# Loading r and k by feature in two transfers of 48 partitions

## The chip, the cores and the metric

The kernel runs on one core of one Trainium2 chip. The metric is device time of the whole kernel in microseconds (us): the median of several executions, and, for the profile, one execution recorded instruction by instruction. PE is TensorE (matrix products), PEld its weight loads, DVE VectorE, ACT ScalarE, POOL GpSimd, SP the engine that issues most of the transfers (DMAs); SPq is SP's queue.

## The reference

Three blocks run one after the other on 3,072 tokens (4 sequences of 768, 8 heads of 48 features, so 384 features per token).

```
# attention, for every sequence and head, t = 0..767, state starts at 0 (48 x 48)
y[t]  = r[t] @ (state + outer(u * k[t], v[t]))
state = w[:, None] * state + outer(k[t], v[t])

# mixture of experts: one of 8 experts per token
e = argmax(x @ w_gate);  p = softmax(x @ w_gate)[e];  g = sigmoid(x @ w_output_gate)[e]
x = p * g * (relu(x @ w1[e]) @ w2[e])          # 384 -> 1024 -> 384

# gated feed-forward
out = (silu(x @ w_gate2) * (x @ w_val)) @ w_out # 384 -> 1536 -> 384
```

## The kernel before

The attention works on 24 tiles of 128 tokens (6 per sequence). Within a tile it uses the form with powers of the decay: r is multiplied by powers of w, k by their inverses, and matrix products give the scores of all pairs of tokens of the tile; a 48 x 48 state per head carries over to the next tile.

For that, each tile needs r and k in two layouts. By token: partition = token, free axis = head and feature (`tok`, 384 KB of r and k per tile, line 342; v is loaded apart, line 346). By feature: partition = feature, free axis = pair of heads and token (`tr`, line 341). Two heads share the 128 partitions: head 0 of a pair has partitions 0 to 47, head 1 partitions 64 to 111. Partitions 48 to 63 and 112 to 127 are rows of zeros, written on the host into `tr`, so that a half always has 64 rows. The products read all 64 rows of a half (lines 496 and 552), so these rows must be zero, not merely unused.

The inputs of a tile land in one of three buffers, `io[i % NIO]` with `NIO = 3`; v has four buffers of its own. `load(i + NIO)` is called in `scaled_r(i)`, as soon as tile i's r and k have been read for the last time.

In this stage the order of every engine's work is the order in which the code is written (`manual_schedule`), SP's too. One round of the loop issues, among others: on POOL `ck` (two products, lines 455 and 456), `kdT` (line 458) and `kdc` (line 460); on DVE `rdT` (line 467), the sums `cb` from `ck` (line 479), the masked copy of the scores (line 500), the state (line 528), and pieces of the routing of the experts (lines 131 to 273); on ACT the diagonal blocks `dsb` (line 483) and copies; on SP the loads of a later tile, the store of the finished rows `x_d` (line 127), and in some rounds weights of the first expert (lines 1050 and 1054), which ACT and DVE split in two parts (lines 1062 and 1065). After the stage come the experts and the feed-forward, ordered by a planner from estimated times.

Of the kernel before, what the change touches and what calls it, by code (L numbers as in the profile page):

```python
# [20 lines left out]
P = 128  # L21
# [17 lines left out]
def moe_kernel(ctx, tc, cst, small, tok, tr, u, w1, w2, m_gate, m_val, m_out, out):  # L39
    nc = tc.nc  # L40
    NT, DM = out.shape
    H, D = u.shape
# [35 lines left out]
    rows = const.tile([P, E * NJ], I32, name="rows")  # L78
# [227 lines left out]
    with ExitStack() as actx:  # L306
# [26 lines left out]
        RK, V, T = 2 * H * D, H * 64, NP * P  # L333
        NIO, NV = 3, 4
# [3 lines left out]
        def load(i):  # L338
            if i < NTILE:
                t = io[i % NIO]  # L340
                nc.sync.dma_start(out=t[:, RK:], in_=tr[i])
                nc.sync.dma_start(out=t[:, 0:RK], in_=tok[i, :, 0:RK])

        def load_v(i):
# [8 lines left out]

        u_tok = carve(H * D).rearrange("p (h d) -> p h d", d=D)
        load(0)
        nc.sync.dma_start(out=u_tok, in_=u.rearrange("(o h) d -> o h d", o=1).to_broadcast([P, H, D]))
        nc.sync.dma_start(out=cs, in_=cst)
        for i in range(1, NIO):
            load(i)
            load_v(i - 1)  # L360
# [101 lines left out]
        def scaled_r(i):  # L462
            if i >= NTILE:
                return
            r_t, k_t, rT, kT, rdT, kdT, ck, kdc = S[i]
            if i:
                nc.vector.tensor_tensor(out=rdT, in0=rT, in1=wr_ps, op=ALU.mult)
            if i == 1:
                load_v(3)
            load(i + NIO)  # L470
            if i == 0:
                load_v(2)
# [1065 lines left out]
```

## Time and profile before

| | us |
|---|---|
| median of 3 runs | 815.05 |
| lowest and highest of them | 812.76, 816.62 |
| the profiled execution, device time | 815.9 |
| its span, first to last instruction | 814.1 |
| TensorE busy in the span | 780.3 |
| VectorE busy | 509.8 |
| GpSimd busy | 206.9 |

The profiled execution is one of its own, so sums over its rows are compared with its 815.9 us. Busy shares are means over stages that differ: the attention fills about the first 126 us, the experts follow to some 360 us, then the feed-forward. A DMA share is the mean busy share of the core's 16 DMA engines; it can come out slightly above 1.

### The profile page before, as it was taken

What the parts mean: (1) busy time and instruction counts of PE and PEld (TensorE: products, weight loads), DVE (VectorE), ACT (ScalarE), POOL (GpSimd) and SP (SyncE); (2) the same over time, 40 slices, a digit from 0 to 9 for tenths busy, and PEclk for the clock granted to TensorE, in tenths of its full rate; (3) what the DMA queues carried; (4) which work ended last, traced back from release to release, by engine and by line L of the source; (5) the groups of instructions that cost most, each with busy time, mean ns of one, the idle gap of its engine ahead of it and who ended that gap; (6) DMA issues with size and microseconds to landing.
All of it is one profiled execution on the core that took longest, in us unless ns stands there. A gap on an engine that the chain in (4) does not pass through costs nothing.

```text
span 814.1 us, 15597 instructions
## 1 busy us (share of the span) xinstructions
PE 780.3 (96%) x5982; PEld 716.5 (88%) x5983; DVE 509.8 (63%) x1091; ACT 347.9 (43%) x791; POOL 206.9 (25%) x203
## 2 busy tenths in 40 slices
PE   6999879699999999999999999999999999999997
PEld 3888778599999999998888888888888888899997
DVE  7799997288999899879564335333533533344443
ACT  5878763275665666565432112222221221222321
POOL 6999951345323422221002000200010020001000
PEclk9999999799999999999999999999999999999999
DMA  8899933665778777454311000000000010001000
GB/s 319 311 355 349 333 129 115 218 211 160 235 261 258 239 240 231 129 179 155 109 38 43 10 1 14 39 1 0 14 40 1 5 42 1 1 8 40 1 20 24
DMA packets 61859, 99.27 MB, mean 122 GB/s; under 512 B 5461, under 2 KB 48105, under 8 KB 61776
## 3 DMA queue, kind: packets, MB, share of 16 engines
q1 hardware_dynamic: 58320, 88.34, 32.9%
q0 software_dynamic: 3456, 9.85, 3.6%
q8 instruction: 49, 0.80, 0.4%
q14 instruction: 34, 0.28, 0.1%
HBM read 81.64 MB, written 16.53 MB: 121 GB/s over the span
## 4 chain that ended last, share of the span: by engine, by line
issue 52%; PE 23%; POOL 3%; DVE 2%; DMA 1%; another core or an unknown queue 1%; ACT 1%; POOLq 0%; SPq 0%; ACTq 0%; DVEq 0%
PE ph L1190 9%; PE py L1190 9%; POOL out_dram L1362 2%; PE pt L1156 1%; DMA rw<-m 1%; PE pha L1190 1%; PE ph L1186 1%; PE pya L1190 1%; POOL x L1033 1%; PE py L1186 1%; DMA m<-x 0%; POOLq L1379 0%; PE ph L1187 0%; DVE wl L968 0%
## 5 line engine op out<-in xcount | busy, mean ns | idle before, releaser
L1386 PE MATMUL pg<-x,wh 128*128 128x512 f32 (+1 forms) x504 | 146.5, 358 | 0.0
L1391 DVE TENSOR_TENSOR hv<-pg,hv 128x512 f32<-128x512 f32 (+1 forms) x84 | 51.6, 614 | 143.2 <-ACT hv L1390 143.0
L1386 PE MATMUL pv<-x,wh 128*128 128x512 f32 (+1 forms) x504 | 137.7, 358 | 0.0
L1362 POOL DMA_INDIRECT out_dram<-ot,tokd x24 | 24.9, 1037 | 407.3 <-DVE ot L1361 402.9
L1390 ACT ACTIVATE hv<-pg 128x512 f32<-128x512 f32 (+1 forms) x84 | 45.0, 536 | 160.1 <-PE pg L1386 159.7
L967 ACT CAST hh<-hv 128x512 fp32r<-128x512 f32 (+1 forms) x84 | 47.0, 560 | 136.0 <-DVE hv L1392 136.0
L1386 PEld LDWEIGHTS pv<-x,wh 128*128 128x128 f32 x504 | 89.9, 188 | 13.9
L1386 PEld LDWEIGHTS pg<-x,wh 128*128 128x128 f32 x504 | 90.2, 188 | 11.3
L1353 PE MATMUL po<-wh,hl 128*128 128x384 f32 x288 | 97.1, 338 | 0.0
L1353 PE MATMUL po<-wl,hh 128*128 128x384 f32 x288 | 96.8, 336 | 0.0
L1353 PE MATMUL po<-wh,hh 128*128 128x384 f32 x288 | 96.8, 336 | 0.0
L1386 PE MATMUL pg<-x,wl 128*128 128x512 f32 (+1 forms) x252 | 90.3, 358 | 0.0
L1386 PE MATMUL pv<-x,wl 128*128 128x512 f32 (+1 forms) x252 | 90.3, 358 | 0.0
L1190 PE MATMUL ph<-x,w1h 128*128 128x416 f32 (+6 forms) x336 | 87.4, 340 | 0.0
L1190 PE MATMUL py<-h,w2h 128*128 128x416 f32 (+6 forms) x336 | 83.0, 341 | 0.0
L968 DVE TENSOR_TENSOR hl<-hv,hh 128x512 fp32r<-128x512 f32 (+1 forms) x84 | 51.7, 615 | 43.9 <-ACT hh L967 43.6
L1392 DVE TENSOR_TENSOR hv<-pv,hv 128x512 f32<-128x512 f32 (+1 forms) x84 | 51.7, 615 | 39.0 <-PE pv L1386 38.6
L483 ACT ACTIVATE dsb<-cs,cb 128x128 f32<-128x128 f32 x192 | 58.8, 389 | 21.0 <-DVE cb L479 21.0
L1190 PEld LDWEIGHTS ph<-x,w1h 128*128 128x128 f32 x336 | 61.4, 188 | 0.1
L1190 PEld LDWEIGHTS py<-h,w2h 128*128 128x128 f32 x336 | 60.7, 188 | 0.5 <-DVE h L1210 0.3
L1190 PE MATMUL ph<-x,w1l 128*128 128x416 f32 (+6 forms) x168 | 58.3, 347 | 0.4 <-DVE h L1210 0.4
L1033 POOL TENSOR_TENSOR low<-low,exw 128x384 f32<-128x384 f32 x30 | 33.5, 1118 | 96.1 <-DVE exw L1029 78.7
(248 smaller groups left out, 1511.2 us busy)
## 6 DMA issues: line engine op xcount, KB each, us to landing
r<-in_w_dram SPq DMA_DIRECT2D x64, 384.0 KB
yd_all<-in_tr_dram SPq DMA_DIRECT2D x24, 512.0 KB
yd_all<-in_tok_dram SPq DMA_DIRECT2D x24, 384.0 KB
rw<-m SPq DMA_DIRECT2D x36, 192.0 KB
yd_all<-in_tok_dram SPq DMA_DIRECT2D x24, 256.0 KB
m<-ab SPq DMA_DIRECT2D x30, 192.0 KB
x_d<-xt SPq DMA_DIRECT2D x24, 192.0 KB
cva<-in_w_gate_dram SPq DMA_DIRECT2D x10, 384.0 KB
```

The source lines that it names most:

```text
L483: nc.scalar.mul(dsb[:, h, :], ident, cb[:, h : h + 1])
L967: first = nc.scalar.copy(hi, src)
L968: second = nc.vector.tensor_tensor(out=lo, in0=src, in1=hi.bitcast(F32), op=ALU.subtract)
L1033: nc.gpsimd.tensor_tensor(out=low, in0=low, in1=ex.bitcast(F32), op=ALU.mult)
L1186: nc.tensor.matmul(dst[:, 0 : 2 * n], lhsT=hi, rhs=x, start=start, stop=False, skip_group_check=True)
L1190: nc.tensor.matmul(dst[:, 0:n], lhsT=a, rhs=b, start=start and t == 0, stop=stop and t == 2)
L1353: mm = nc.tensor.matmul(po[t], lhsT=a[:, t * P : (t + 1) * P], rhs=bb, start=(f == 0 and j == 0), stop=(f == KF2 - 1 and j == 2))
L1362: st = nc.gpsimd.indirect_dma_start(out=out[:, :], out_offset=bass.IndirectOffsetOnAxis(ap=tokd[:, i : i + 1].bitcast(U32), axis=0), in_=o ...
L1386: nc.tensor.matmul(dst, lhsT=a[:, fs], rhs=bb[:, q, :], start=(q == 0 and j == 0), stop=(q == KD - 1 and j == 2))
L1390: nc.scalar.activation(hv, pg, AF.Sigmoid)
L1391: nc.vector.tensor_tensor(out=hv, in0=pg, in1=hv, op=ALU.mult)
L1392: nc.vector.tensor_tensor(out=hv, in0=pv, in1=hv, op=ALU.mult)
```

## The change

The loads of r and k by feature of the first three tiles, which are the first to fill each of the three buffers, stay as they were and bring the zero rows. From the fourth tile on, the load is issued as two: partitions 0 to 47 and partitions 64 to 111. The rows of zeros are then not loaded again; they stay in the buffers. Nothing else in the program is edited.

```
         def load(i):
             if i < NTILE:
                 t = io[i % NIO]
-                nc.sync.dma_start(out=t[:, RK:], in_=tr[i])
+                rows = [slice(0, P)] if i < NIO else [slice(0, D), slice(P // 2, P // 2 + D)]
+                for pr in rows:
+                    nc.sync.dma_start(out=t[pr, RK:], in_=tr[i, pr])
                 nc.sync.dma_start(out=t[:, 0:RK], in_=tok[i, :, 0:RK])
```

Here P is 128 and D is 48.

## Rows read from the trace of the kernel before

**Rows 1.** The page, the span in 40 slices of 20.4 us, busy tenths.

```profile
DVE  7799997288999899879564335333533533344443
DMA  8899933665778777454311000000000010001000
```

**Rows 2.** Busy time by stretch; last three columns granted clock, DMA share, GB/s.

```profile
10.00:40.00 30.00, 24.31 (x483) 21.78 (x482) 24.07 (x59) 23.43 (x74) 28.66 (x31) 0.94 0.94 341
40.00:90.00 50.00, 45.17 (x1030) 40.24 (x1028) 47.24 (x139) 40.28 (x124) 46.69 (x45) 1.00 1.00 359
90.00:110.00 20.00, 16.82 (x354) 14.45 (x351) 19.24 (x58) 15.53 (x48) 18.03 (x16) 1.00 0.80 270
110.00:126.00 16.00, 13.07 (x299) 11.71 (x293) 14.34 (x53) 9.07 (x29) 4.02 (x4) 1.00 0.22 68
148.00:157.00 9.00, 1.09 (x8) 0.89 (x7) 0.00 (x0) 1.02 (x3) 5.25 (x7) 0.74 1.04 374
...
55.00:60.00 5.00, 4.11 (x92) 3.67 (x92) 4.90 (x18) 3.59 (x11) 4.28 (x5) 1.00 1.05 413
```

**Rows 3.** Waits of POOL from 55 to 126 us: total, times, longest.

```profile
POOL ck L455 <- DMA yd_all<-in_tok_dram: 3.7, 5, 1.3
```

**Rows 4.** Waits of DVE, first 40 to 55 us, then 55 to 126 us.

```profile
DVE cb L479 <- POOL ck L456: 1.2, 3, 0.5
...
DVE bank L241 <- ACT eo L237: 1.2, 3, 0.4
DVE x L968 <- ACT x L967: 0.9, 1, 0.9
DVE cb L479 <- POOL ck L456: 0.5, 1, 0.5
```

**Rows 5.** Timeline of POOL: start, duration, instruction (tiles 12, 17, 18, 23).

```profile
56.35 1.00 POOL L455 TENSOR_TENSOR ck<-yd_all 128x384 f32<-128x384 f32 x1 [0.64 <-DMA yd_all<-in_tok_dram]
57.43 1.00 POOL L456 TENSOR_TENSOR ck<-ck,yd_all 128x384 f32<-128x384 f32 x1
...
80.08 1.01 POOL L456 TENSOR_TENSOR ck<-ck,yd_all 128x384 f32<-128x384 f32 x1
...
83.58 1.00 POOL L455 TENSOR_TENSOR ck<-yd_all 128x384 f32<-128x384 f32 x1 [1.26 <-DMA yd_all<-in_tok_dram]
84.66 1.00 POOL L456 TENSOR_TENSOR ck<-ck,yd_all 128x384 f32<-128x384 f32 x1
...
108.56 1.00 POOL L455 TENSOR_TENSOR ck<-yd_all 128x384 f32<-128x384 f32 x1 [1.00 <-DMA yd_all<-in_tok_dram]
109.63 1.01 POOL L456 TENSOR_TENSOR ck<-ck,yd_all 128x384 f32<-128x384 f32 x1
```

**Rows 6.** Timeline of DVE: "cb" of tiles 11, 12, 17, 18, 23.

```profile
54.51 0.55 DVE L479 TENSOR_REDUCE cb<-ck 128x8 f32<-128x384 f32 x1 [0.50 <-POOL ck L456]
...
60.41 0.55 DVE L479 TENSOR_REDUCE cb<-ck 128x8 f32<-128x384 f32 x1
...
83.78 0.54 DVE L479 TENSOR_REDUCE cb<-ck 128x8 f32<-128x384 f32 x1
...
91.22 0.54 DVE L479 TENSOR_REDUCE cb<-ck 128x8 f32<-128x384 f32 x1
...
115.94 0.55 DVE L479 TENSOR_REDUCE cb<-ck 128x8 f32<-128x384 f32 x1
```

**Rows 7.** First piece of the chain of waits that ended last.

```profile
128.29 0.85 issue
```

**Rows 8.** DMA issues of r and k by feature, with size.

```profile
yd_all<-in_tr_dram SPq DMA_DIRECT2D x24, 512.0 KB
```

**Rows 9.** Timeline of SP's queue: two issues of a load by feature.

```profile
70.57 0.33 SPq L341 DMA_DIRECT2D yd_all<-in_tr_dram  x1
...
75.92 1.82 SPq L341 DMA_DIRECT2D yd_all<-in_tr_dram  x1
```

**Rows 10.** Longest wait of SP's queue up to 130 us.

```profile
SPq L127 <- ACT lh L129: 49.9, 22, 6.1
```

## Prediction

> **What bounds the kernel now.** I read the page's slices first, then busy time by stretch, then who waited for whom, then single instructions. The edit touches only the loads of the attention stage, so the reader is to see there which engine sets the pace and whether a late load reaches it.
>
> The slices [rows 1] show DMA at 8 or 9 tenths in the first five slices (to about 102 us), and little of it in the last half. In finer stretches [rows 2] the 16 DMA engines are busy 0.94 of 10 to 40 us, 1.00 of 40 to 90 us, and 0.80 of 90 to 110 us. At first sight the stage is short of DMA, and taking bytes away should help.
>
> But full DMA engines need not be what the end waits for. GpSimd (POOL) is the first reader of a tile's loads. From 55 to 126 us it waited for a load 5 times, 3.7 us in all [rows 3]. VectorE (DVE) stands behind POOL: its row sum "cb" (L479) reads the "ck" that POOL made. DVE is busy 47.24 of the 50 us from 40 to 90, 19.24 of the next 20 and 14.34 of the next 16 [rows 2]. Its own waits in 55 to 126 us are 0.5 us for POOL, 1.2 and 0.9 us for ScalarE (ACT), and none for a load [rows 4]. The one wait for POOL ended at 54.51 [rows 6], before the first late load (tile 12, whose POOL work began at 56.35 after 0.64 us of waiting [rows 5]).
>
> So from about 55 us to the end of the stage DVE runs its list without a stop, and POOL is ahead of it. How far ahead is read from one tile in both lists [rows 5, 6]. Counting L456 and L479 along the tiles:
> - tile 12: POOL ends at 57.43 + 1.00 = 58.43, DVE takes it up at 60.41: 1.98 us spare, after a load that came 0.64 late.
> - tile 17: 80.08 + 1.01 = 81.09 against 83.78: 2.69 spare, its load not late.
> - tile 18: 84.66 + 1.00 = 85.66 against 91.22: 5.56 spare, after the latest load of all (1.26).
> - tile 23: 109.63 + 1.01 = 110.64 against 115.94: 5.30 spare, after 1.00.
>
> Every late load of the kernel before dies in this spare time. The chain of waits itself begins only at 128.29 [rows 7], after the stage, and doesn't reach back; the argument therefore rests on DVE's list.
>
> **The change, part by part.**
>
> *Bytes.* One load of r and k by feature is 512 KB [rows 8], 128 rows of 4 KB. Two of 48 rows carry 384 KB: 128 KB (131,072 bytes) less in each of the 21 tiles from the fourth on, 2.75 MB in all. At 413 GB/s, the rate of 55 to 60 us at full DMA [rows 2], 512 KB take 1.27 us and 128 KB 0.32 us. If time went by bytes, the stage would need 21 x 0.32 = 6.7 us less of DMA time. What it is worth to the end: POOL would lose some or all of its 3.7 us of waiting, and DVE, which waits for none of it, would gain 0. Earlier than 55 us POOL never waits for one of the changed loads, so there is nothing to gain either. The term is 0.
>
> *One more transfer per tile.* SP issues 21 instructions more. An issue takes 0.33 us when SP is free, at worst 1.82 [rows 9]. Queued behind it on SP are the tile's token load (r and k by token), the v load and the store of x. The token load is what POOL asks for first, so it starts 0.33 us later, at worst 1.82. SP has the time: it stood 49.9 us before the store of x (L127) waiting for ACT [rows 10]. A token load that is so much later is a fixed delay, not one that adds up, and the smallest spare above is 1.98 us. The cost is 0; without that cover it would be 0.33 us once (at worst 1.82), as DVE would run that much later throughout. The two halves also write the same buffer that the one load wrote, so they wait for the same readers, and the readers now wait for two arrivals in place of one. The rows that aren't loaded keep the zeros that the first three tiles brought.
>
> *How fast a transfer to 48 partitions runs.* Every load of this stage that the trace shows fills 128 partitions; none shows 48. I bound it. Let x be what a tile's two halves together take of DMA time beyond the 1.27 us of the whole one. Lower end: by bytes, x = -0.32. Upper end: each half, although it carries 3/8 of the bytes, holds the engines as long as the whole load did, x = +1.27. The nearest row is the whole load itself: same 4 KB rows, same source and queue, only fewer of them; by it a transfer goes by its rows, and I take a value in the lower part of the range, between -0.32 and the middle (+0.48).
>
> [...]
>
> *What x costs.* From tile 3 to tile n the DMA engines owe (n - 2) times x more. Idle DMA time pays back: 0.06 x 30 = 1.8 us in 10 to 40 us, 0 in 40 to 90, 0.20 x 20 = 4.0 us in 90 to 110 [rows 2]. What is left goes first into DVE's spare time. So DVE is late by
> - tile 12: 10x - 1.8 - 1.98 = 10x - 3.8;
> - tile 17: 15x - 1.8 - 2.69 = 15x - 4.5;
> - tile 23: 21x - 5.8 - 5.30 = 21x - 11.1.
> (The spares above were measured after the late loads, so those are in them.) DVE has no idle time to make good what it loses, so the largest of these counts. At x = -0.32 all are below 0, cost 0. At the middle, 0.48: 1.0, 2.7 and below 0. At 1.27: 8.9, 14.6 and 15.6 us. To come to 4.1 us (0.5% of 815, about what a measurement of this kernel can tell from no change), x must be (4.1 + 4.5)/15 = 0.57.
>
> **Sum.** Bytes 0, issue 0, x in the lower part of its range 0. The profiled execution took 815.9 us for a span of 814.1, with 1.8 us around it; so 815.9 - 0 on its own scale. It stands 0.85 us above the median of the runs, 815.05, so I forecast 815.0.
>
> **The rivals.**
>
> *Slower: the halves are slow.* Place: the DMA engines between 40 and 90 us, share 1.00, no idle time there. Mechanism: a half writes fewer partitions, so if what limits a load is the side that takes the data, 16 engines push into half of it. For it: engines that are equally full move different amounts (359 GB/s at share 1.00 in 40 to 90 us, 413 at 1.05 in 55 to 60 us [rows 2]), so bytes alone don't set a transfer's time. Against it: nothing in the trace has such a shape. It decides from x = 0.57 on. In the middle of 0.57 and 1.27, at 0.92, tile 17 gives 15 x 0.92 - 4.5 = 9.3 us: 824.4 us; at its worst 815.05 + 15.6 = 830.7. [...]
>
> *Faster: POOL sets the pace after all.* DVE's few waits for POOL between 40 and 55 us sum to 1.2 us [rows 4]; if loads were behind these too, and all 3.7 us of POOL's waiting for loads came through to the end, the gain would be 4.9 us: 810.2 us. Against it: those three waits come before any late load, and from 55 us on DVE has work in hand. This is the largest gain I can find.
>
> *The change does nothing that can be seen, although it does what it says.* This is my forecast, not a rival; DMA share falls and DVE's list ends when it did. Within it, a gain of up to 1.2 us or a loss at x up to 0.57 is possible: 811 to 819 us.
>
> *The work after the stage moves.* [...] The edit moves no load of that stretch, so I give it no chance of its own, only part of the ends.
>
> **How the numbers follow.** My forecast 0.57 (811 to 819 us). Halves slow enough to decide 0.34 (819 to 831): no row supports it, but no row excludes it, and the threshold lies at 0.57 in a range up to 1.27. Faster by over 4.1 us 0.09. For 8 in 10 I leave out 0.07 below and 0.13 above: 812 to 826 us; the upper end is x of about 1.0 (15 x 1.0 - 4.5 = 10.5). Faster 0.09, within 0.5% 0.57, slower 0.34.
>
> **What would show it.** Right: POOL's waits for loads below 3.7 us, DMA share of 40 to 90 us below 1.00, about 0.92 by bytes (11 tiles x 0.32 = 3.5 us of 50), bytes moved down by 2.75 MB; DVE's idle time in 55 to 126 us as before, and its last "cb" at about 115.9 us. Wrong through slow halves: DMA share still 1.00 while GB/s fall below 359, POOL's waits for loads of 10 us and more, DVE waiting for POOL in tiles 12 to 17, last "cb" later than 119 us. Wrong through a gain: last "cb" before 112 us. If the last "cb" stays and the time moves, it is the stretch after the stage.

## Result and the profile after

The changed kernel is slower: 818.96 us (median of 10 runs, 816.51 to 822.01) against 813.23 us (10 runs, 810.90 to 816.62) on the same chip. The ratio is 1.0068, 95% interval 1.0051 to 1.0084, so some 5.5 us (4 to 7). I had forecast 815.0, with a chance of 0.57 on no change. The time lies inside the range (812 to 826), but on the rival's side of the 0.5%: "the halves are slow".

The profiled execution took 819.2 us for a span of 817.4. Its line numbers are two higher from the edit on (L455 is now L457, L479 is L481). First the page: the DMA slices of 20.4 us, the packets of the whole execution, and the queue that SP's loads use.

```profile
DMA  8999953665687778365311000000000010001000
GB/s 280 283 299 305 294 176 117 229 196 171 213 281 228 248 230 260 110 190 155 99 57 43 10 1 14 39 1 0 14 39 1 3 43 1 1 8 40 1 20 24
DMA packets 61523, 96.52 MB, mean 118 GB/s; under 512 B 5797, under 2 KB 48441, under 8 KB 61440
...
q1 hardware_dynamic: 57984, 85.59, 34.2%
```

The kernel before had:

```profile
DMA packets 61859, 99.27 MB, mean 122 GB/s; under 512 B 5461, under 2 KB 48105, under 8 KB 61776
...
q1 hardware_dynamic: 58320, 88.34, 32.9%
```

The 2.75 MB are gone as worked out, yet the engines are no less busy: in the sixth slice (102 to 123 us), which holds the end of the loads, DMA now shows 5 tenths against 3 [rows 1]. The busy time by stretch says it plainly (columns as in [rows 2]):

```profile
10.00:40.00 30.00, 25.63 (x520) 23.01 (x524) 23.80 (x60) 23.02 (x75) 28.02 (x30) 0.94 1.04 296
40.00:90.00 50.00, 45.55 (x971) 40.23 (x963) 43.79 (x131) 39.82 (x122) 41.91 (x40) 0.97 1.05 300
90.00:110.00 20.00, 17.09 (x343) 14.92 (x342) 19.42 (x50) 13.94 (x44) 19.04 (x17) 0.91 1.06 297
110.00:126.00 16.00, 11.94 (x257) 10.72 (x259) 15.05 (x60) 9.40 (x32) 9.28 (x9) 1.00 0.35 110
```

From 40 to 90 us the engines are full (1.05, before 1.00) and carry 300 GB/s in place of 359. The idle DMA time that was to pay back, 0.06 of 10 to 40 us and 0.20 of 90 to 110 us [rows 2], is gone. DVE is busy 43.79 of the 50 us, before 47.24.

Who waited for whom, POOL and then DVE, from 55 to 126 us (total, times, longest):

```profile
POOL ck L457 <- DVE bank L210: 2.9, 1, 2.9
POOL ck L457 <- DVE lg L131: 2.7, 1, 2.7
POOL ck L457 <- DMA yd_all<-in_tok_dram: 1.8, 2, 1.1
...
DVE cb L481 <- POOL ck L458: 2.4, 4, 1.4
```

DVE waits 2.4 us for POOL, before 0.5 [rows 4]. By the names in this list POOL's waits for loads went down, 3.7 us [rows 3] to 1.8, and POOL now waits for DVE. The names mislead here. Two waits of POOL, in tiles 12 and 18:

```profile
58.98 0.99 POOL L457 TENSOR_TENSOR ck<-yd_all 128x384 f32<-128x384 f32 x1 [2.66 <-DVE lg L131]
...
89.98 0.99 POOL L457 TENSOR_TENSOR ck<-yd_all 128x384 f32<-128x384 f32 x1 [2.87 <-DVE bank L210]
```

The rows name DVE, which signals after nearly every instruction (1,038 signals, 1,091 instructions in this execution) and did so at 58.91 and 89.95 us, just ahead of the two starts. But all that "ck" needs from DVE is the buffer of the "ck" two tiles earlier, and DVE had read that by 51.60 and 81.62 us. The token loads of the two tiles landed at 58.85 and 89.85 us (times of their signals in the trace), and POOL began 0.13 us behind each. It began 0.13 us behind the landing in tiles 15 and 21 too, whose waits are named for the load. So all of these were waits for loads, and so was one of 0.65 us in tile 16. Counted by landings, POOL waited 8.0 us for loads from 55 to 126 us, before 4.0.

DVE's "cb" of tiles 11, 12, 15, 16, 17, 18 and 23:

```profile
55.13 0.56 DVE L481 TENSOR_REDUCE cb<-ck 128x8 f32<-128x384 f32 x1 [0.46 <-POOL ck L458]
61.09 0.55 DVE L481 TENSOR_REDUCE cb<-ck 128x8 f32<-128x384 f32 x1
...
76.14 0.55 DVE L481 TENSOR_REDUCE cb<-ck 128x8 f32<-128x384 f32 x1 [1.38 <-POOL ck L458]
81.07 0.55 DVE L481 TENSOR_REDUCE cb<-ck 128x8 f32<-128x384 f32 x1 [0.42 <-POOL ck L458]
85.91 0.55 DVE L481 TENSOR_REDUCE cb<-ck 128x8 f32<-128x384 f32 x1 [0.18 <-POOL ck L458]
93.38 0.54 DVE L481 TENSOR_REDUCE cb<-ck 128x8 f32<-128x384 f32 x1
...
119.12 0.55 DVE L481 TENSOR_REDUCE cb<-ck 128x8 f32<-128x384 f32 x1
```

The last one starts at 119.12, before 115.94 [rows 6]: 3.18 us late. The span is 3.3 us longer, so in this pair of executions the stage accounts for all of it, and nothing is added behind the stage. (The pair shows less than the medians: the kernel before's execution, 815.9 us, was 2.7 us above its later median of 813.23.)

The durations of the packets on queue q1 in the first 126 us, read from the trace by size, show where the engines' time went. In this stretch the 4 KB packets are the loads by feature, 3 KB the token loads and 2 KB the loads of v; the edit touches only the first. The sum of the durations is divided by the 16 engines:

```
packet bytes   before: mean ns, sum us    after: mean ns, sum us
4096           184, 35.2                  221, 33.2
3072           134, 25.6                  182, 34.9
2048            88, 16.9                  113, 21.7
```

The loads by feature themselves took 2.0 us less in all, with the halves, than before. The 9.3 and 4.8 us more fell on the token loads and the loads of v, which run beside them.

### The profile page after: what moved, and what is told of

Its sections match the earlier page's. It is cut to its first block, busy times and chain, and to the rows that moved or that the text cites. A ratio compares the mean times of both kernels' runs of the same rounds, so it can differ in the third digit from the quotient of the medians.

```text
span 817.4 us, 15634 instructions
## 1 busy us (share of the span) xinstructions
PE 784.2 (96%) x5982; PEld 719.3 (88%) x5983; DVE 510.2 (62%) x1091; ACT 348.2 (43%) x791; POOL 208.4 (25%) x203
## 3 DMA queue, kind: packets, MB, share of 16 engines
q1 hardware_dynamic: 57984, 85.59, 34.2%
## 4 chain that ended last, share of the span: by engine, by line
issue 53%; PE 14%; DVE 6%; POOL 4%; DMA 3%; ACT 2%; another core or an unknown queue 1%; POOLq 0%; SPq 0%; ACTq 0%; DVEq 0%
PE ph L1192 5%; PE py L1192 5%; POOL out_dram L1364 2%; DMA m<-ab 1%; DMA rw<-m 1%; PE pha L1192 1%; DVE ab L1038 1%; PE pya L1192 1%; PE ph L1188 1%; POOL xg L1144 1%; PE pt L1158 1%; DVE w2l L1067 1%; DVE low L1037 1%; DVE w1l L1067 1%
```

## The experiments

They ran on three other chips: the probe and the three kernels behind it (halves of 64, column halves, fewer bytes) on one where the kernel before took 805.57 us; the changed kernel once more, halves from tile 12 on, the token load first and 112 partitions on one with 806.33; the kernel before with its trace and halves in tiles 3 to 11 on one with 805.77. A ratio is always to the kernel before on the same chip. Theory A, an assumption: a transfer's time goes by how its partitions lie, and that makes a half slow. Theory B: two transfers cost more than one, whatever they fill. Later theory C: only the order on SP's queue hurts.

### The disputed cost by itself

A kernel that does nothing of the computation and writes zeros: 14 groups (the first a warm-up) of 20 loads, or pairs of loads, from the array by feature into 20 separate buffers, each group ended by a DVE sum over all buffers, which waits for the group's loads.

```diff
+group("g_128", (slice(0, P), full))
+group("g_48_48", (slice(0, 48), full), (slice(64, 112), full))
+group("g_64_64", (slice(0, 64), full), (slice(64, 128), full))
+group("g_cols", (slice(0, P), slice(0, 512)), (slice(0, P), slice(512, W)))
+group("g_128x3k", (slice(0, P), slice(0, 768)))
+group("g_112", (slice(0, 112), full))
...
+group("g_48_at0", (slice(0, 48), full))
+group("g_48_at40", (slice(40, 88), full))
+group("g_64_at0", (slice(0, 64), full))
+group("g_64_at32", (slice(32, 96), full))
```

> This kernel does no attention, experts or feed-forward; it only loads: 13 groups of 20 transfers (or pairs) from the array of r and k by feature, each group ended by a DVE sum over what it brought, and then stores zeros. [...] Theory B (a second transfer has a fixed price, 0.88 us in the profile after): 48 + 48, 64 + 64 and the two column halves each cost 0.88 us more than their bytes (1.8, 2.15, 2.15), and the first partition makes no difference.

The timeline of DVE; the number in brackets is the wait for a group's 20 loads. In order: 128 rows, 48+48, 64+64, two halves of the columns, 128 rows of 3 KB, 112 rows from partition 0, 96 from 0, 96 from 16, 48 from 0, 48 from 40, 64 from 0, 64 from 32, 128 rows again (2% more than the first time).

```profile
74.14 0.28 DVE L54 TENSOR_REDUCE g<-buf 128x20 f32<-128x80 f32 x1 [27.79 <-DMA buf<-in_tr_dram]
114.12 0.29 DVE L54 TENSOR_REDUCE g<-buf 128x20 f32<-128x80 f32 x1 [39.70 <-DMA buf<-in_tr_dram]
162.49 0.28 DVE L54 TENSOR_REDUCE g<-buf 128x20 f32<-128x80 f32 x1 [48.08 <-DMA buf<-in_tr_dram]
193.72 0.28 DVE L54 TENSOR_REDUCE g_cols<-buf 128x20 f32<-128x80 f32 x1 [30.95 <-DMA buf<-in_tr_dram]
218.04 0.28 DVE L54 TENSOR_REDUCE g_128x3k<-buf 128x20 f32<-128x80 f32 x1 [24.04 <-DMA buf<-in_tr_dram]
256.51 0.28 DVE L54 TENSOR_REDUCE g<-buf 128x20 f32<-128x80 f32 x1 [38.18 <-DMA buf<-in_tr_dram]
287.72 0.29 DVE L54 TENSOR_REDUCE g<-buf 128x20 f32<-128x80 f32 x1 [30.93 <-DMA buf<-in_tr_dram]
317.44 0.29 DVE L54 TENSOR_REDUCE g<-buf 128x20 f32<-128x80 f32 x1 [29.43 <-DMA buf<-in_tr_dram]
344.07 0.28 DVE L54 TENSOR_REDUCE g_at<-buf 128x20 f32<-128x80 f32 x1 [26.34 <-DMA buf<-in_tr_dram]
360.28 0.29 DVE L54 TENSOR_REDUCE g_at<-buf 128x20 f32<-128x80 f32 x1 [15.93 <-DMA buf<-in_tr_dram]
388.45 0.28 DVE L54 TENSOR_REDUCE g_at<-buf 128x20 f32<-128x80 f32 x1 [27.88 <-DMA buf<-in_tr_dram]
406.27 0.29 DVE L54 TENSOR_REDUCE g_at<-buf 128x20 f32<-128x80 f32 x1 [17.53 <-DMA buf<-in_tr_dram]
434.89 0.28 DVE L54 TENSOR_REDUCE g_128b<-buf 128x20 f32<-128x80 f32 x1 [28.34 <-DMA buf<-in_tr_dram]
```

Two halves of 48 rows take (39.70 - 27.79)/20 = 0.60 us more than the whole load with its 33% more bytes: x = 0.60. For 64+64 it is 1.01, for two transfers that both fill 128 partitions 0.16. So theory B carries about a quarter of the loss (0.16 of 0.60). Among five of the groups what decides is where the rows lie: 48 rows cost 26.34 us from partition 0 and 15.93 from partition 40; 64 rows 27.88 from 0 and 17.53 from 32; and 48, 64 or 128 rows from partition 0 take about the same, 26.34, 27.88 and 27.79. The rows that are read move along with the partitions here, so the probe alone doesn't tell the place in SBUF from the place in DRAM. Theory A has the direction; the sizes don't follow the bytes: 48 rows from partition 0 took 1.32 us each and rows of 3 KB 1.20, where three eighths and three quarters of the whole load's 1.39 are 0.52 and 1.04.

The first partition doesn't explain all of them: 96 rows (30.93 from partition 0, 29.43 from 16) and 112 rows (38.18) took longer than 128 rows (27.79). And the second half of a pair is not free: 20 pairs of 64-row halves moved twice the bytes of 20 halves from partition 0 alone in 48.08 against 27.88 us, 16% more per time, 20 pairs of 48 rows 33% more per time (39.70 against 26.34).

### Same split, other shapes, in the kernel

Two halves of 64 partitions (the bytes of before):

```diff
-rows = [slice(0, P)] if i < NIO else [slice(0, D), slice(P // 2, P // 2 + D)]
+rows = [slice(0, P)] if i < NIO else [slice(0, P // 2), slice(P // 2, P)]
```

> From the fourth tile on two transfers of 64 partitions, pads included: the bytes of the kernel before. Theory A: at the 215 GB/s that the 48-row halves come to, x = 2 x 1.22 - 1.27 = 1.17, by the formula 15 x 1.17 - 4.5 = 13 us slower than before, about 826 us, 64-row halves clearly worse than 48-row ones. Theory B: 0.88 us per second transfer, x = 0.88, 8.7 us slower, 822 us.

823.22 us, ratio 1.0251 (1.0227 to 1.0275), about 20 us: slower than either theory had it. Waits of POOL from 40 to 130 us, and the last "cb":

```profile
POOL ck L457 <- DMA yd_all<-in_tok_dram: 13.6, 6, 4.0
POOL ck L457 <- DVE st L530: 4.3, 1, 4.3
...
132.88 0.55 DVE L481 TENSOR_REDUCE cb<-ck 128x8 f32<-128x384 f32 x1
```

Even by the names POOL's waits for loads are 13.6 us here. Counted by landings over the whole stage they are 24.7 us; in the changed kernel they were 8.9, in the kernel before 4.0, in the column kernel, which follows, 2.5.

Two transfers of 128 partitions, each half the columns:

```diff
-nc.sync.dma_start(out=t[:, RK:], in_=tr[i])
+cols = [slice(0, 2 * T)] if i < NIO else [slice(0, T), slice(T, 2 * T)]
+for c in cols:
+    nc.sync.dma_start(out=t[:, RK + c.start : RK + c.stop], in_=tr[i, :, c])
```

> From the fourth tile on two transfers of 128 partitions, 2 KB of each row apiece: as many transfers, waits and issues as after, all partitions, the bytes of before. Theory A: within 2 us of before (813), DVE hardly waits for POOL. Theory B: x = 0.88, 8.7 us slower, 822 us.

806.62 us, ratio 1.0009 (0.9998 to 1.0020): no loss from the 21 additional transfers that could be told from noise. Stretches:

```profile
40.00:90.00 50.00, 45.16 (x980) 40.06 (x978) 46.14 (x137) 38.82 (x119) 46.84 (x44) 0.98 1.00 357
90.00:110.00 20.00, 18.23 (x385) 15.86 (x383) 19.25 (x59) 16.79 (x53) 19.37 (x18) 0.97 0.80 269
```

These are the rows of before again (1.00 and 359, 0.80 and 270, [rows 2]). Theory B falls.

One transfer of 128 partitions that leaves out the last quarter of the columns, so the 384 KB of the change; the output is another one, and tokens go to other experts:

```diff
+c = slice(0, 2 * T if i < NIO else 3 * T // 2)
+nc.sync.dma_start(out=t[:, RK + c.start : RK + c.stop], in_=tr[i, :, c])
```

> From the fourth tile on one transfer of 128 partitions that leaves out the last quarter of each row, so part of r and k of two pairs of heads is of an earlier tile, and the tokens may go to other experts: only the attention stage is to be read. It moves the 384 KB of after in one full transfer. If the bytes are worth nothing to the end, as the prediction has it: DMA share of 40 to 90 us about 0.92, POOL waits for loads below 1 us, and DVE's last cb still at 115 to 117 us. If late loads did hold DVE up: last cb 1 to 5 us earlier than the 115.9 of before.

Its whole time (975.47 us) can't be read for that reason; its attention stage can. DMA share from 40 to 90 us fell to 0.95 (0.92 expected), POOL's waits for loads were 1.8 us by landings (2.5 in the column kernel), and the last "cb" started at 114.74, no earlier than in the column kernel (114.23). Bytes saved in transfers that stay fast gain nothing: that term of 0 was right.

### Where in the stage the loss arises

> The changed kernel once more, on the chip of the next three, to have them side by side. Every theory expects what was measured before, a ratio near 1.007 (1.0051 to 1.0084) to the kernel before, and the last row sum cb of the stage about 3 us later than in the kernel before.

The changed kernel: 809.82 us, ratio 1.0050 (1.0032 to 1.0068).

> The kernel before, once more with its trace, on the chip of the experiments. The kernel with two column halves, on this chip, had its last cb at 114.23 us and a time ratio of 1.0009; if it may stand for the kernel before, the last cb here is at 114 to 116 us and tile 5 at 29 to 31 us.

The kernel before: one run of 805.47 us, last "cb" at 114.49, tile 5 at 29.46. It serves as the reference for the starts of "cb" on the other chips too (the three medians of the kernel before are within 0.8 us). All these starts are of one execution each.

Halves only from tile 12 on, then only in tiles 3 to 11:

```diff
-rows = [slice(0, P)] if i < NIO else [slice(0, D), slice(P // 2, P // 2 + D)]
+rows = [slice(0, P)] if i < 12 else [slice(0, D), slice(P // 2, P // 2 + D)]
...
+rows = [slice(0, P)] if i < NIO or i >= 12 else [slice(0, D), slice(P // 2, P // 2 + D)]
```

> Halves only from tile 12 on: 12 tiles instead of 21. With x = 0.60 the DMA engines owe 7.2 us more. By the formula of the prediction (DVE's spare time takes it up, idle DMA time of 90 to 110 us pays 4.0): tile 17 is late by 6 x 0.60 - 2.69 = 0.9 us, tile 23 by nothing; at most 1 us, ratio 1.000 to 1.001. If the spare time isn't independent (a late DVE frees buffers late, so the next loads and POOL start late too): 2 to 3 us, ratio 1.002 to 1.004. If the loss were spread evenly over the tiles, 12/21 of 5.7 us: 3.3 us, 1.004.

> Halves in tiles 3 to 11 only; whole loads from tile 12 on: the part that the kernel with halves from tile 12 on leaves out. If tiles lose each by itself (the loss goes wherever a late load meets no spare time), this part makes up the rest of the whole loss: 1.0050 - 1.0033 to 1.0068 - 1.0033, that is 1.4 to 2.8 us, ratio 1.002 to 1.0035, with the step at tiles 4 and 5, before DVE has spare time. By the formula of the prediction, at x = 0.60: 9 x 0.60 - 1.8 - 1.98 = 1.6 us at tile 12 and no more behind it, ratio 1.002. If the early tiles are harmless, since POOL has caught up by 55 us, 0 us and ratio 1.000, and the whole loss needs both parts together.

From tile 12 on: 807.75 us, 1.0033 (1.0017 to 1.0049). Tiles 3 to 11: 808.05 us, 1.0028 (1.0015 to 1.0042). Start of "cb", read from the four timelines of DVE, with how much later than in the kernel before:

| tile | before | all tiles | 3 to 11 | from 12 |
|---|---|---|---|---|
| 4 | 25.96 | 26.28 (+0.3) | 26.36 (+0.4) | 25.13 (-0.8) |
| 5 | 29.46 | 31.98 (+2.5) | 31.82 (+2.4) | 29.56 (+0.1) |
| 11 | 53.68 | 56.46 (+2.8) | 56.30 (+2.6) | 54.08 (+0.4) |
| 14 | 69.64 | 73.14 (+3.5) | 71.80 (+2.2) | 69.69 (+0.1) |
| 15 | 73.40 | 76.92 (+3.5) | 75.56 (+2.2) | 74.89 (+1.5) |
| 21 | 103.56 | 107.71 (+4.2) | 105.92 (+2.4) | 105.66 (+2.1) |
| 23 | 114.49 | 118.62 (+4.1) | 116.83 (+2.3) | 116.56 (+2.1) |

The two parts add up, 2.34 + 2.07 = 4.41 us against 4.13. In that kernel tiles 3 to 11 lose their whole share by tile 5 and never get it back. Its timeline of POOL (tiles 3 and 4) and of DVE (tile 5):

```profile
18.26 1.00 POOL L457 TENSOR_TENSOR ck<-yd_all 128x384 f32<-128x384 f32 x1 [1.04 <-DVE st L525]
...
24.03 1.00 POOL L457 TENSOR_TENSOR ck<-yd_all 128x384 f32<-128x384 f32 x1 [1.49 <-DMA yd_all<-in_tok_dram]
...
31.82 0.55 DVE L481 TENSOR_REDUCE cb<-ck 128x8 f32<-128x384 f32 x1 [2.04 <-POOL ck L458]
```

The token loads of tiles 3 and 4, each issued behind halves, are late for POOL by 1.04 and 1.49 us (the first wait, too, ended 0.16 us behind the load's landing at 18.10). From there to tile 11 POOL has no idle time: it starts a tile's "ck" every 4.25 us from tile 6 on, here from 32.98 to 54.18, in the kernel before from 30.31 to 51.56. So the 2.7 us stay, and DVE stands 2.04 us for POOL at tile 5 (0.99 in the column kernel). How much is lost there differs from execution to execution: in the profiled pair of the result the same two waits were 0.29 and 0.67 us, "cb" of tile 11 was 0.6 us late (55.13 against 54.51 [rows 6]), and most of the 3.18 us came from tile 15 on. With halves from tile 12 on, the loss comes at tile 15:

```profile
72.77 1.01 POOL L457 TENSOR_TENSOR ck<-yd_all 128x384 f32<-128x384 f32 x1 [2.80 <-DMA yd_all<-in_tok_dram]
...
74.89 0.55 DVE L481 TENSOR_REDUCE cb<-ck 128x8 f32<-128x384 f32 x1 [1.37 <-POOL ck L458]
```

SP issues that tile's loads directly behind two weight loads of 384 KB (L1052, L1056), as it does for tiles 12, 18 and 21. POOL began it at 67.97 in the column kernel and at 69.88 in the kernel before, both without a wait for a load: 4.8 and 2.9 us earlier.

### The order on the queue

The token load, which POOL reads first, is issued ahead of the two halves:

```diff
+nc.sync.dma_start(out=t[:, 0:RK], in_=tok[i, :, 0:RK])
 rows = [slice(0, P)] if i < NIO else [slice(0, D), slice(P // 2, P // 2 + D)]
 for pr in rows:
     nc.sync.dma_start(out=t[pr, RK:], in_=tr[i, pr])
-nc.sync.dma_start(out=t[:, 0:RK], in_=tok[i, :, 0:RK])
```

> The token load is issued ahead of the two halves. Theory A (the halves hold the DMA engines longer, and it is that time which is short): the order on the queue changes little, ratio 1.005 to 1.008 as for the changed kernel. Theory C (POOL reads the token load first, and what costs is only that this load comes later behind two slower transfers): most of the loss goes, ratio 1.000 to 1.003.

810.67 us, 1.0063 (1.0046 to 1.0079). Theory C falls. The waits go elsewhere:

```profile
DVE dsb L502 <- PE pss L498: 5.2, 5, 2.1
DVE rdT L469 <- DMA yd_all<-in_tr_dram: 1.3, 1, 1.3
...
DVE cb L481 <- POOL ck L458: 0.5, 2, 0.3
```

DVE (40 to 130 us) hardly waits for POOL any more, but for the halves themselves (rdT) and for TensorE, whose "pss" needs what is made of them. The DMA share is 1.04 from 40 to 90 us all the same: the time is short on the DMA engines, and the order changes who waits.

### One transfer, 112 partitions

```diff
+pr = slice(0, P if i < NIO else P // 2 + D)
+nc.sync.dma_start(out=t[pr, RK:], in_=tr[i, pr])
```

> One transfer of 112 partitions from the fourth tile on, 448 KB. Theory A (what a transfer costs goes by the partitions that it fills and how they lie): by the probe 20 such loads took 38.18 us against 27.79, x = 0.52, almost the 0.60 of the two halves, so slower by about 4 to 5 us, ratio 1.004 to 1.007. Theory B (two transfers cost more than one): no loss, ratio 1.000. By bytes (one eighth fewer): 1.000 or below.

813.68 us, 1.0096 (1.0072 to 1.0119): about 7.7 us, the last "cb" at 122.21. One transfer per tile, and an eighth fewer bytes than before, cost more than the two halves. The number of transfers and the bytes are out as causes once more. But the size is more than the 4 to 5 us that I worked out from the probe, and why 112 partitions are this slow isn't settled: in the probe, too, 20 such loads took 38.18 us, and 20 of 128 partitions 27.79.

No experiment points to a version that beats the kernel before: at full speed the fewer bytes gain nothing (114.74 against 114.23). A layout whose rows lie otherwise on the partitions was not tried in the kernel.

## Why the prediction was wrong

**The step that failed** is "How fast a transfer to 48 partitions runs", where I took "a value in the lower part of the range", because the nearest row was the whole load and a transfer would go "by its rows". x is 0.60 in the probe (20 pairs of halves took 39.70 us, 20 whole loads 27.79). In the kernel, all of queue q1's packets together took 34.2% of 817.4 us against 32.9% of 814.1 before, 11.7 us of engine time over 21 tiles: 0.56, from shares rounded to 0.1%. This is the upper half of my range (-0.32 to 1.27), at the threshold of 0.57. Neither the number of rows nor the bytes set the time alone; where the rows lie counts too: in the probe 20 loads of 48 rows took 26.34 us from partition 0 and 15.93 from partition 40. And x isn't a time of the halves alone, as the step had it: their own packets took 2.0 us less in all, and the token loads and the loads of v 14.1 us more. In the second pair, on the other chips, it is 1.5 us less and 13.8 us more.

**The formula gave about the right sum for partly wrong reasons.** With x = 0.60 it yields 15 x 0.60 - 4.5 = 4.5 us; measured are 4.1 us of stage and a ratio of 1.0050 on one chip, 3.2 us of stage in the profiled pair and 1.0068 in the medians on the other. But it lets spare time and idle DMA time be subtracted from the debt of all tiles. For halves from tile 12 on it gives 0.9 us, measured are 2.1 us of stage and a ratio that is at least 1.0017. It looked only at tiles 12, 17, 18 and 23. Before tile 12 there is no spare: POOL is busy 28.66 of the 30 us from 10 to 40 [rows 2], and DVE stood 0.50 us for POOL at tile 11 [rows 6], and 1.2 us from 40 to 55 us [rows 4]. That POOL never waits for a load there I read as "nothing to gain"; it also meant that a late load would go straight through, as tiles 3 to 5 show. And with halves from tile 12 on, tile 15 began later than the debt of tiles 12 to 15 accounts for (2.9 to 4.8 us against 4 x 0.60 = 2.4). At 64+64 the formula falls short too (15 x 1.01 - 4.5 = 10.7 us against 18.4 of stage, 132.88 - 114.49); which of the two is the reason there no run shows.

**Bytes, 0; one more transfer, 0**: right (384 KB in full-width transfers, 114.74; column halves, 1.0009).

**The rivals.** "The halves are slow" is what happened, at the low end of what I gave it (819 to 831), but its mechanism, the side that takes the data, was not shown: the probe doesn't tell it from the place that is read. "POOL sets the pace after all" held from tile 5 to tile 11, where it cost rather than gained. The stretch behind the stage moved with the stage and added nothing in the profiled pair.

**The signs.** GB/s below 359 at a full DMA share (300 at 1.05), DVE waiting for POOL between tiles 12 and 17 (1.38, 0.42 and 0.18 us in tiles 15 to 17), and the last "cb" after 119 us: all came. "POOL's waits for loads of 10 us and more" did not quite: 8.0 us by landings, twice the 4.0 of before. By the profile's names they were 1.8 us, which would have met "below 3.7", my sign for being right, while the kernel lost.

**Open**: why four halved tiles make tile 15's start 2.9 to 4.8 us late when 4 x 0.60 is 2.4; why most of the price falls on the token loads; and why 112 partitions take longer than 128 (38.18 against 27.79 us in the probe).

## What to carry to other kernels

Before rows are cut from a load, ask how the rest lies on the partitions: a load that skips unused partitions can take longer than one that brings them along (39.70 us for 20 pairs of 48 rows, 27.79 for 20 whole loads), and 48 rows from partition 0 cost nearly as much here (26.34) as 128. Where the first reader of a load has no idle time (POOL in tiles 5 to 11), a late load goes straight through (with halves in tiles 3 to 11 "cb" was 2.4 us late at tile 5 and 2.6 at tile 11); so read the spare time at every tile from the first changed one on, not at the tiles that were late before. A wait that the profile puts down to a busy engine can be a wait for a load (2.66 and 2.87 us here, named for DVE): ask what the instruction needs from that engine and since when it was there, before a sum of waits is read as a success. And look for the price of a slow transfer in the transfers beside it (14.1 us more there, 2.0 us less in the halves themselves).

## What the runs showed of the hardware that was not expected

- 20 loads of the same 48 rows of 4 KB took 26.34 us from partition 0 and 15.93 from partition 40.
- 20 loads of 112 rows took 38.18 us, more than 128 rows (27.79) and 96 rows (30.93); in the kernel 112 rows cost 1.0096.
- Beside the halves the packets of other loads took longer: in the attention stage 3 KB packets from a mean of 134 to 182 ns, 2 KB from 88 to 113. In engine time that was 9.3 and 4.8 us more, with 2.0 us less for the halves themselves.
- In the kernel, two loads of 128 partitions and half the columns cost no more than one whole load (1.0009, 0.9998 to 1.0020).
